# A bias laid into PSUM by ScalarE, and a 64-row product issued into both halves of the array

## The chip, the cores and the metric

The kernel runs on one core of a Trainium2 chip. The core has TensorE (PE: matmuls; its weight loads are the rows PEld), VectorE (DVE), ScalarE (ACT), GpSimd (POOL) and SyncE (SP, which here issues all DMAs). The metric is the device time of one execution in microseconds (us), as the median of the runs: 431.13 us before the change.

## What is computed

Eight batches of 576 rows. An attention through 32 learned memories gives x; x goes through a gated MLP whose gate is mixed over the rows of the sequence by a 576 x 576 matrix and gets a bias per row:

```python
attn_out = softmax(scale * q @ k_m.T) @ v_m            # k_m, v_m: 32 memories per head
x = attn_out.transpose(0, 2, 1, 3).reshape(8, 576, 512)
h = relu(x @ w_in);  u, v = h[..., :512], h[..., 512:]
v_n = (v - mean(v)) / sqrt(var(v) + 1e-6)              # over the 512 columns
v_s = einsum('ts,bsd->btd', w_spatial, v_n) + b_spatial[None, :, None]
out = (u * v_s) @ w_out
```

The change is in the line of `v_s`, the spatial product, and in the order in which all work is issued.

## The kernel before

**Precision.** The large products are made of a high and a low part of each operand (hi x hi, hi x lo, lo x hi), each part in a 32-bit format that TensorE streams in one pass. So a product costs three matmuls where one would be written. Tiles with the suffix h or l (`vh`, `vl`, `wth`, `wtl`, `gh`, `gl`, `woh`, `wol`) are such parts.

**Stages of a batch.** Every stage is a Python generator, and each `yield` ends one step. A letter names the stage:

- P (`memory_weights`) and K (`memories`) make the memories of the batch; S (`scores`) the attention weights `ah`, `al`; Q loads and turns the queries; M (`products`) multiplies the memories by w_in and gives `mh`, `ml`.
- V (`gate`, five row tiles) makes the rows of v, normalises them and leaves `vh`, `vl`. The last tile has only 64 rows (`SR`): its high part goes into rows 0 to 63 of `t1`, its low part into rows 64 to 127 of `t1`, and its high part once more into rows 0 to 63 of `t2`.
- U (`units`, four column tiles of 128) makes u. Each takes 12 matmuls of 288 columns into one double bank of PSUM.
- G (`spatial`, four column tiles) makes the spatial product into a double bank `ps`: the 576 output columns stand as 2 x 288, one half (`hf`) in each bank. Over four tiles of 128 rows stand 3 products x 2 halves = 24 matmuls. The 64 rows that remain take two products of 128 rows each: (`t1`, `ws1`) is hi x hi and lo x hi at once, since `ws1` holds the transposed weights twice; (`t2`, `ws2`) is hi x lo in rows 0 to 63, and in rows 64 to 127 the bias: `t2` is all ones there and `ws2` holds the bias's high part in row 64 and its low part in row 96, zeros elsewhere. That makes 28 matmuls a tile. The first starts the accumulation (`start=(n == 0)`). DVE then multiplies u by `ps` (line 689), and ACT and DVE split the product into `gh`, `gl` and the 64 remaining rows' `grh`, `grl`.
- O (`project`) multiplies by w_out: 12 matmuls of 512 columns a tile; the 64 remaining rows of two batches go together in every second batch.

Steps that happen once: D loads w_in (64-bit floats, which `decode` turns to 32 bits in the stages E and L), X does the same with w_out (`prepare_out`), W loads w_spatial (`load_spatial`), T transposes it on TensorE (`transpose_spatial`; its fifth tile, T4, fills `ws1` and `ws2`), and B (`prepare_bias`) puts the bias into `ws2`.

**Order.** Nothing is scheduled by the compiler: `START` and `PLAN` are lists of letters, each a step of its stage, and every engine runs its instructions in that order (`tc.manual_schedule`). `START` is written out once, for the first batch; `PLAN` is repeated for batches 1 to 7, and a prime means the next batch, two primes the one after. An engine whose next instruction waits therefore holds up all that stands behind it.

**PSUM.** `ps1` has four single banks, `ps2` two double banks. All tiles `pu` and `ps` share the two double banks, so a G tile can start only when an earlier tile's bank has been read out, by ACT (u, line 649) or by DVE (g, line 689).

**Shapes on TensorE.** The profile names a matmul by the rows and columns of the array that it uses. Most are 128\*128 (or 128\*64 for V's last tile). K, S and M use eight small tiles of 64\*32 at once, in both halves of the rows and in four groups of columns. A matmul of plain 32-bit floats in K, S and M shows as two instructions in the trace. A matmul with 64 rows and 128 columns (64\*128) stands only in T, where the last 64 rows of w_spatial are transposed (line 287).

Of the kernel before, what the change touches and what calls it, by code (L numbers as in the profile page):

```python
# [39 lines left out]

PLAN = """
    U0 P'*3 K' P' V1 V0 U0 K' U0 K' V2 U2 V0 V1*3 U1 V2 V0 V2 V0 V4 U1 V1 V0 V2 K' Q' P'' V1 U1
    V3 U3 Q' U2 V1 V4*2 K' V2 P'' K'*2 P'' V3 P'' K' P'' V3 V4 K' K'' U3 K' S' U2 U3 V2 V4 S' V3
    S' V3 S'*2 G0 V4 G1 P'' M0' Q'' P'' M1' M0' S' V3 V2 S' M1'*2 G0 V4 G1 G0 V3 S' G1 V4 G0 P''
    M1' S' M0' Q G1 G0 M1' G0 S' G1 S' M1' K'' P'' G0 S' Q'' G1 G0*2 M0' G2 G3 P'' G2 S' G3 G1*3
    G2 G3 G2*3 M1' G3 O3 G2 S' G3 S'*2 O0 G3 S' O1 G3 O0 S' G3 P'' M0' S' O3 O0 G2 O0 G3 O1 O3
    M0' O3 O4 G2 Q'' O2 M0' O1 O4 O1 V0' O2 O4*2 Q'' O2 V0' O2
"""

ON_VECTOR = set(  # L50
# [7 lines left out]
def memory_attention_spatial_gate(  # L58
# [75 lines left out]
    nc.gpsimd.memset(t2[SR:P, :].bitcast(F32), 1.0)  # L134
# [5 lines left out]
    ws2 = const.tile([P, S], F32R, name="ws2")  # L140

    state = {}

# [6 lines left out]
    def tensor_unless(name):  # L150
        return None if name in ON_VECTOR else nc.tensor
# [81 lines left out]
        yield from decode(w, state["raw", c][n], w, power, f"{'LE'[c]}{n}")  # L233

    def prepare_out(b, j):
        place = two.tile([P, 1, 3 * DM], I32, tag="raw_out", name="raw_out")
        raw, f = place[:, :, 0 : 2 * DM], place[:, :, 2 * DM :].bitcast(F32)
        nc.sync.dma_start(raw[:, 0], w_out[j * P : (j + 1) * P].bitcast(I32))
        yield
        power = two.tile([P, 1, DM], I32, tag="o", name="power")  # L240
        yield from decode(None, raw, f, power, f"X{j}")
        if ("wo", j // 2) not in state:
            state["wo", j // 2] = tuple(
                one.tile([P, 2, DM], F32R, tag=f"{part}{j // 2}", name=part)
                for part in ("woh", "wol")
            )
        woh, wol = (x[:, j % 2] for x in state["wo", j // 2])
        w = raw.rearrange("p j (f t) -> p j f t", t=2)[:, 0, :, 1].bitcast(F32)
        nc.scalar.copy(woh, w)
        yield  # L250
        engine(f"X{j}.wol").tensor_tensor(wol, w, woh.bitcast(F32), op=ALU.subtract)
        yield

    def load_spatial(b, _):
        w_sb = one.tile([P, NI, S], F32, tag="u", name="w_sb")
        w_rem = two.tile([SR, S], F32, tag="g", name="w_rem")
        b_sb = two.tile([P, S], F32, tag="g", name="b_sb")
        state["spatial"] = w_sb, w_rem, b_sb
        nc.gpsimd.memset(b_sb[SR:P], 0.0)
        nc.sync.dma_start(w_sb, w_spatial[0:SM].rearrange("(i p) s -> p i s", i=NI))  # L260
        nc.sync.dma_start(w_rem, w_spatial[SM:S])
        for r in (64, 96):
            nc.sync.dma_start(b_sb[r : r + 1], b_spatial.rearrange("(o s) -> o s", o=1))
        yield
        w_dup = one.tile([P, NI, 2, SR], F32, tag="grh", name="w_dup")
        w_rem_dup = one.tile([SR, 2, SR], F32, tag="grl", name="w_rem_dup")
        state["dup"] = w_dup, w_rem_dup
        for c in range(2):
            nc.scalar.copy(w_dup[:, :, c, :], w_sb[:, :, SM:S])
            yield  # L270
            nc.scalar.copy(w_rem_dup[:, c, :], w_rem[:, SM:S])
            yield

    def transpose_spatial(b, si):
        w_sb, w_rem, _ = state["spatial"]
# [29 lines left out]
    def prepare_bias(b, _):  # L305

        b_sb = state["spatial"][2]
        nc.scalar.copy(ws2[SR:P], b_sb[SR:P])
        yield
        nc.gpsimd.tensor_tensor(  # L310
            ws2[96:97], b_sb[96:97], ws2[96:97].bitcast(F32), op=ALU.subtract
        )
        yield


    def over_rows(eng, to, op):

# [257 lines left out]
    def gate(b, st):  # L575
# [78 lines left out]
    def spatial(b, dt):  # L654
# [10 lines left out]
        rc = slice((b % 2) * SR, (b % 2 + 1) * SR)  # L665
        ps = banks(f"ps_{b}_{dt}")
        cs = slice(dt * P, (dt + 1) * P)
        ops = []
        for i in range(NI):
            ops += [  # L670
# [1 line left out]
                (vh[:, i, cs], wtl[:, i, :]),  # L672
                (vl[:, i, cs], wth[:, i, :]),
            ]
        ops += [(t1[:, cs], ws1), (t2[:, cs], ws2)]
        for n, (a, w) in enumerate(ops):
            for hf in range(2):
                nc.tensor.matmul(  # L678
                    ps[:, hf, 0:HALF],
                    a,  # L680
                    w[:, hf * HALF : (hf + 1) * HALF],
                    start=(n == 0),
                    stop=(n == len(ops) - 1),
                )
            if n in (2, 5, 8):
                yield
# [47 lines left out]
    def warm_up(b, _):  # L734
# [76 lines left out]
```

## Time and profile before

| | before |
|---|---|
| time, median of 3 runs (lowest, highest) | 431.13 us (431.1, 431.83) |
| span of the profiled execution, first to last instruction | 429.2 us |
| PE busy | 399.7 us, 3844 matmuls |
| DVE busy | 292.5 us |
| ACT busy | 228.3 us |
| POOL busy | 81.7 us |
| bytes moved by DMA | 50.69 MB |

The profile gives the span of one execution; the device time of that same execution is not listed beside it. The runs' median is 1.9 us longer than the span, which is what lies before the first and after the last instruction.

How to read it: the page's first part gives busy time, but matmuls are pipelined, and the end of a matmul is modelled, so a PE that is "busy" is not shown to be at its peak. What tells more is the distance between the starts of two matmuls of a stream. In the timeline, neighbouring instructions of one kind are merged into a row: start, time to the end of the last, engine, line, operation, output<-inputs, shape, count. A bracket at the end is idle time of the engine before the row and what ended it. A group's row gives busy time and the mean of one in ns.

### The profile page before, as it was taken

How to read it: one execution, taken by the hardware profiler on the slowest of the kernel's cores; microseconds unless marked ns; L12 is line 12 of the kernel's file. 1: busy time of each engine (PE TensorE's matmuls, PEld its weight loads, DVE VectorE, ACT ScalarE, POOL GpSimd, SP SyncE). 2: the span in 40 equal slices, each digit the busy share in tenths (PEclk: the TensorE clock that was granted, in tenths of full speed). 3: DMA queues.
4: the chain of work that ended last, by engine and by line, in shares of the span. 5: the costliest groups of instructions: out<-in, count | busy, mean ns of one | idle time of the engine just before them, and what ended most of it. 6: DMA issues, size and time to landing. Idle time of an engine off the chain costs nothing.

```text
span 429.2 us, 9278 instructions
## 1 busy us (share of the span) xinstructions
PE 399.7 (93%) x3844; PEld 335.9 (78%) x3844; DVE 292.5 (68%) x536; ACT 228.3 (53%) x438; POOL 81.7 (19%) x154
## 2 busy tenths in 40 slices
PE   3176799999999999999999999999999999999996
PEld 2063487988798887988798887988798888988984
DVE  3699999994997358953897168955897069824420
ACT  2657697654845277245835176245825276337422
POOL 1344353332300031023200030003200040005000
PEclk9999699999999999999999999999999999999999
DMA  8989639217960369014941279025911200020003
GB/s 291 401 296 323 78 99 225 108 48 178 224 93 25 100 197 185 8 73 141 240 34 43 83 210 178 0 76 185 199 30 58 67 2 0 2 98 2 0 2 121
DMA packets 85790, 50.69 MB, mean 118 GB/s; under 512 B 66226, under 2 KB 70322, under 8 KB 85748
## 3 DMA queue, kind: packets, MB, share of 16 engines
q1 hardware_dynamic: 85748, 50.10, 45.3%
q8 instruction: 30, 0.49, 0.5%
q14 instruction: 12, 0.10, 0.1%
HBM read 40.65 MB, written 9.44 MB: 117 GB/s over the span
## 4 chain that ended last, share of the span: by engine, by line
PE 89%; DVE 4%; DMA 3%; ACT 2%; issue 1%; SPq 0%; ACTq 0%; DVEq 0%
PE ps L678 29%; PE po L718 23%; PE pv L591 14%; PE pu L640 12%; PE kvm L375 4%; PE mp L561 4%; PE sc L492 2%; DMA raw<-in_moe_w_in_dram 2%; DMA w_rem<-in_moe_w_spatial_dram 2%; DVE win_sb L218 1%; DVE power L210 1%; DVE sm L512 1%; ACT raw L208 1%; ACT qT L445 0%; DVE g L689 0%
## 5 line engine op out<-in xcount | busy, mean ns | idle before, releaser
L598 DVE BATCH_NORM_STATS2 st<-vr 128x6 f32<-128x512 f32 (+1 forms) x40 | 27.4, 686 | 46.6 <-ACT vr L595 46.6
L678 PE MATMUL ps<-wth,vh 128*128 128x288 f32 x256 | 57.8, 307 | 0.1
L603 POOL TENSOR_SCALAR rs<-mv 128x1 f32<-128x1 f32 (+1 forms) x40 | 11.6, 291 | 236.1 <-DVE mv L600 232.1
L700 ACT CAST gh<-g 128x512 fp32r<-128x512 f32 x32 | 19.9, 621 | 67.9 <-DVE g L689 67.9
L678 PE MATMUL ps<-wtl,vh 128*128 128x288 f32 x256 | 54.9, 296 | 0.0
L678 PE MATMUL ps<-wth,vl 128*128 128x288 f32 x256 | 54.7, 295 | 0.0
L718 PE MATMUL po<-woh,gh 128*128 128x512 f32 x128 | 50.5, 394 | 0.0
L718 PE MATMUL po<-wol,gh 128*128 128x512 f32 x128 | 50.4, 394 | 0.0
L718 PE MATMUL po<-woh,gl 128*128 128x512 f32 x128 | 50.3, 393 | 0.0
L678 PEld LDWEIGHTS ps<-wth,vh 128*128 128x128 f32 x256 | 40.6, 188 | 11.0 <-issue 5.5
L724 ACT COPY o<-po 128x512 f32<-128x512 f32 x36 | 21.1, 587 | 51.5 <-PE po L718 51.5
L678 PEld LDWEIGHTS ps<-wtl,vh 128*128 128x128 f32 x256 | 41.3, 188 | 0.0
L678 PEld LDWEIGHTS ps<-wth,vl 128*128 128x128 f32 x256 | 41.3, 188 | 0.0
L613 ACT ACTIVATE vr<-vr,sh,rs 128x512 f32<-128x512 f32 (+1 forms) x40 | 32.4, 815 | 2.6 <-POOL sh L608 2.3
L591 PE MATMUL pv<-mh,ah 128*128 128x512 f32 (+1 forms) x80 | 32.9, 411 | 0.0
L649 ACT ACTIVATE u<-pu 128x576 f32<-128x576 f32 x32 | 20.2, 659 | 21.8 <-PE pu L640 21.5
L595 ACT ACTIVATE vr<-pv 128x512 f32<-128x512 f32 (+1 forms) x40 | 23.8, 595 | 14.6 <-PE pv L591 14.6
L591 PE MATMUL pv<-ml,ah 128*128 128x512 f32 (+1 forms) x80 | 31.6, 395 | 0.0
L591 PE MATMUL pv<-mh,al 128*128 128x512 f32 (+1 forms) x80 | 31.6, 395 | 0.0
L689 DVE TENSOR_TENSOR g<-u,ps 128x576 f32<-128x576 f32 x32 | 23.9, 750 | 10.8 <-PE ps L678 10.5
L718 PEld LDWEIGHTS po<-woh,gl 128*128 128x128 f32 x128 | 24.0, 188 | 5.7
L718 PEld LDWEIGHTS po<-woh,gh 128*128 128x128 f32 x128 | 24.0, 188 | 5.2
(150 smaller groups left out, 872.2 us busy)
## 6 DMA issues: line engine op xcount, KB each, us to landing
kv_sb<-in_k_dram SPq DMA_DIRECT2D x8, 1152.0 KB, 6.9
kv_sb<-in_v_dram SPq DMA_DIRECT2D x8, 1152.0 KB, 8.9
out_dram<-o SPq DMA_DIRECT2D x32, 256.0 KB, 2.0
q_sb<-in_q_dram SPq DMA_DIRECT2D x28, 288.0 KB, 6.5
phi_sb<-in_phi_dram SPq DMA_DIRECT2D x8, 576.0 KB, 4.1
raw<-in_moe_w_in_dram SPq DMA_DIRECT2D x8, 512.0 KB, 8.1
raw_out<-in_moe_w_out_dram SPq DMA_DIRECT2D x4, 512.0 KB, 3.6
w_sb<-in_moe_w_spatial_dram SPq DMA_DIRECT2D x1, 1152.0 KB, 6.8
```

Source lines behind the costliest of these rows:

```text
L375: nc.tensor.matmul(kvm[r][32 * j : 32 * j + 32], phi_sb[halves[r], j, i, :], kv_sb[halves[r], j, :, i * D : (i + 1) * D], start=(i == 0), ...
L591: nc.tensor.matmul(pv, x[:, r, cs], m[:, r, DM:DFF], start=(n == 0), stop=(n == 5))
L595: nc.scalar.activation(vr, pv, AF.Relu)
L598: nc.vector.bn_stats(st6, vr)
L613: nc.scalar.activation(vr, vr, AF.Identity, bias=sh, scale=rs)
L640: nc.tensor.matmul(pu[:, hf, 0:HALF], m[:, r, cs], a[:, r, hf * HALF : (hf + 1) * HALF], start=(n == 0), stop=(n == 5),)
L649: nc.scalar.activation(u[:, dt, :].rearrange("p (a s) -> p a s", a=2), pu[:, :, 0:HALF], AF.Relu)
L678: nc.tensor.matmul(ps[:, hf, 0:HALF], a, w[:, hf * HALF : (hf + 1) * HALF], start=(n == 0), stop=(n == len(ops) - 1),)
L689: nc.vector.tensor_tensor(g.rearrange("p (a s) -> p a s", a=2), u[:, dt, :].rearrange("p (a s) -> p a s", a=2), ps[:, :, 0:HALF], op=ALU.mult,
L700: nc.scalar.copy(hi, x)
L718: nc.tensor.matmul(po, a, w, start=(n == 0), stop=(n == 11))
L724: nc.scalar.copy(o, po)
```

## The change

Three things, and what they need:

1. **Bias.** The bias is no longer a row of the product. `b_spatial` is loaded into all 128 rows of a new tile `b_all` (a broadcast DMA in `load_spatial`). At the start of each G tile ACT copies it into the double bank, and all matmuls accumulate onto it (`start=False`). The copy is a step of its own. The stage B, the tile `b_sb`, its memset and the memset of ones in `t2` go away.
2. **hi x lo of the remaining 64 rows.** In place of two matmuls of 128 rows with (`t2`, `ws2`), two of 64 rows: half 0 takes rows 0 to 63 of `t1` and `ws2`, half 1 takes rows 64 to 127 of `t2` and `ws2`. `ws2` holds the low part of the weights' left 288 columns in its upper rows and of the right 288 in its lower rows. V's last tile writes `t2` in rows 64 to 127, and T4 writes `ws2` in pieces.
3. **Orders.** `START` and `PLAN` are new. `prepare_out` keeps two buffers for the raw words but only one for `f`.

```diff
@@ spatial
+        nc.scalar.copy(ps[:, :, 0:HALF], b_all.rearrange("p (a s) -> p a s", a=2))
+        yield
         ops = []
...
-        ops += [(t1[:, cs], ws1), (t2[:, cs], ws2)]
-        for n, (a, w) in enumerate(ops):
+        ops += [(t1[:, cs], ws1), None]
+        for n, both in enumerate(ops):
             for hf in range(2):
+                rows = slice(hf * SR, (hf + 1) * SR)
+                if both:
+                    a, w = both[0], both[1][:, hf * HALF : (hf + 1) * HALF]
+                else:
+                    a, w = (t1, t2)[hf][rows, cs], ws2[rows]
                 nc.tensor.matmul(
                     ps[:, hf, 0:HALF],
                     a,
-                    w[:, hf * HALF : (hf + 1) * HALF],
-                    start=(n == 0),
+                    w,
+                    start=False,
                     stop=(n == len(ops) - 1),
+                    skip_group_check=True,
                 )
@@ gate, last tile
-            nc.scalar.copy(t2[0:SR], vr)
+            nc.scalar.copy(t2[SR:P], vr)
@@ load_spatial
-        nc.gpsimd.memset(b_sb[SR:P], 0.0)
...
-        for r in (64, 96):
-            nc.sync.dma_start(b_sb[r : r + 1], b_spatial.rearrange("(o s) -> o s", o=1))
+        nc.sync.dma_start(b_all, b_spatial.rearrange("(o s) -> o s", o=1).to_broadcast([P, S]))
@@ transpose_spatial, T4
-                yield from low(f"wtl{si}{cs.start}", ws2[0:SR, cs], part[0:SR], hi[0:SR])
+                name = f"wtl{si}{cs.start}"
+                if tensor_unless(name):
+                    nc.tensor.matmul(
+                        part, minus, hi, start=False, stop=True, skip_group_check=True
+                    )
+                yield
+                for hf in range(2):
...
+                    if tensor_unless(name):
+                        nc.scalar.copy(to, part[rows, at])
+                    else:
+                        nc.vector.tensor_tensor(
+                            to, part[rows, at], hi[rows, at].bitcast(F32), op=ALU.subtract
+                        )
+                yield
@@ prepare_out
-        place = two.tile([P, 1, 3 * DM], I32, tag="raw_out", name="raw_out")
-        raw, f = place[:, :, 0 : 2 * DM], place[:, :, 2 * DM :].bitcast(F32)
+        raw = two.tile([P, 1, 2 * DM], I32, name="raw_out")
+        f = one.tile([P, 1, DM], F32, name="f_out")
```

Of the orders, the part that a middle batch spends on G and its neighbours, as TensorE meets it when the two lists are read off (x6, x4, x2: matmuls as the kernel writes them; "pair": the two of 64 rows; mb: one transpose of P):

```
before: ... kvm x40, pv1, pu0, kvm x32+8, ... sc, ps0 x6, ps1 x6, mt, mp, mp, ps0 x6, ps1 x6, ps0 x6,
        ps1 x6, ps0 x6+4, ps1 x6+4, mb, ps2 and ps3 in turn by x6, ps2 x6+4, ps3 x6+4, po ...
after:  ... pv1, kvm x40, kvm x32+8, ... ps0 x6, ... sc, ps0 x12, mt, ps1 x12, ps0 x6+2, pair, mp, mp,
        ps1 x6, ps1 x6+2, pair, ps2 x18, ps2 x6+2, pair, mb, ps3 x18, (po1 x6), ps3 x6+2, pair, po ...
```

While `PLAN` runs, the two parts of K stand together in the new order, and the pair of G0 stands directly before M. Over the whole program the lists hold 32 stretches of 64\*32 work before and 25 after, and 32 pairs, of which 6 stand directly before such a stretch.

More of the change, by code (lines that the diff above doesn't have):

```diff
@@ new lines @@
+    T1 T2*2 L1 T1 P L1 E0 L0 P L0 L1 E0 L1 P T2 L1 T0 E0 T4 E0 Q T0 P E0 D1 K*2 L1 T4 X0 Q K*2 L0
+    K*2 Q T4 E0 E1*2 Q*3 P' T4 X0 K Q P' Q*3 E1 K P' K X1 K T0 Q P' Q S E1*2 X0 S*3 M0 P' K' X0 S
+    T0*2 M0 P' T4 P' M0 S M0 P' S E1 P' E1 T4 E1 M0 X0 T4 X0 S P' M0 T3*2 P' K' T3 S T3 M0 T3 M1
+    T3 P' S*3 M1 T0 Q' S M1*2 P' M1 S K' P' M1 P' T0 S K' S T3 S*2 K' U0 S M1 U1 X0*2 V1 Q' V1 V0
+    K' V1 X0 V0 Q' U0 V0 X1 V0 V2 K' Q' K' V3 U0 X0 V2 P'' V1 U1 V0*2 U3 X1 P'' V1 K' V0 V2 X0 X1
+    Q' U1 V4 U2 U3 Q' V1 X1 V1 V4 K' V2 K' V3*3 V4 K' U3 G0 V2 S' U2 P'' S' V2 S'*2 V4 U2 V3 X1
@@ L39 @@
+    G0*2 M0' S' V2 M1' G1 V4 X2 X1*2 M1' X1 G1 V3 V4 P'' X2 X1 G1 X2 V4 G1 V3 M1' V4 X1 X2 G1 X2
+    G0 P'' M1' G1 X2*2 G0 G3 S' X2 X3 P'' M1' G1 P'' M0' M1' K'' Q'' G3 G0 G3*2 G0 G2 X3 G1 G3 X2
+    G1 P'' G0 X3 G2 P'' G2 X3 G0 S' G1 M0' K'' X3 G2 X3 G0 X3 P'' M0' S' M1' X2 X3 P'' G2*3 G3 O3
+    G3 X2 X3*2 G2 M0' X3 G3 S' G3 S' P'' O1 S' G2 O2 O3 S' O3 S'*2 O1 S'*3 O2 M0' O3 P'' M0' O2
+    O0 O2 S'*2 O0 O1 O0 P'' O0 G3 P'' G2 O1
 """
 PLAN = """
[L42 removed]
@@ L48 @@
+    V3 U2 P'' G0 U0 V4 U0 V3 V1 G0 Q' V4 K'*3 U3 V3 V2 V3 V4 Q U3 V3 S' P''*2 K'' U3 Q'' P'' V2
+    P'' V4 V3 G0 S'*2 G1 V4 G0 V4 S' P'' V4 P'' S' G1 V4 G1 G0 M1' M0' S' G0 M0' M1' S' M0' G2 G1
+    G0 G1 P'' G1 S' G1 G0 M0' G2 K'' S' G2 G1 G2 G0 G1 M1'*2 G2 M0' G1 P'' S' G2 G3*4 M1' M0' P''
+    S' G2 O1 G3 O3 G0 M1' G2 S' G3 S' G3*2 G2 O1*2 G3 Q'' M1' O3 S'*2 O3 S' O2 O1 O3 O2 O4 M0' G2
+    S'*3 O0 G3 V0'*2 O2 O4 P'' Q''*2 O0 O2 O0 O4 O0 O4
 """
@@ L133, in memory_attention_spatial_gate @@
     t2 = const.tile([P, 512], F32R, name="t2")
-    nc.gpsimd.memset(t2[SR:P, :].bitcast(F32), 1.0)
+    b_all = const.tile([P, S], F32, name="b_all")
     win_sb = const.tile([P, NJ, DFF], F32, name="win_sb")
@@ L139, in memory_attention_spatial_gate @@
     ws1 = const.tile([P, S], F32R, name="ws1")
-    ws2 = const.tile([P, S], F32R, name="ws2")
+    ws2 = const.tile([P, HALF], F32R, name="ws2")
     state = {}
@@ L256, in load_spatial @@
         w_rem = two.tile([SR, S], F32, tag="g", name="w_rem")
-        b_sb = two.tile([P, S], F32, tag="g", name="b_sb")
-        state["spatial"] = w_sb, w_rem, b_sb
-        nc.gpsimd.memset(b_sb[SR:P], 0.0)
+        state["spatial"] = w_sb, w_rem
         nc.sync.dma_start(w_sb, w_spatial[0:SM].rearrange("(i p) s -> p i s", i=NI))
         nc.sync.dma_start(w_rem, w_spatial[SM:S])
-        for r in (64, 96):
-            nc.sync.dma_start(b_sb[r : r + 1], b_spatial.rearrange("(o s) -> o s", o=1))
+        nc.sync.dma_start(b_all, b_spatial.rearrange("(o s) -> o s", o=1).to_broadcast([P, S]))
         yield
@@ L302, in transpose_spatial @@
             else:
-                yield from low(f"wtl{si}{cs.start}", ws2[0:SR, cs], part[0:SR], hi[0:SR])
[L305 to L313, printed above, removed]
+                name = f"wtl{si}{cs.start}"
[6 more added lines that the diff above has]
+                    rows = slice(hf * SR, (hf + 1) * SR)
+                    first = max(cs.start, hf * HALF)
+                    count = min(cs.stop, (hf + 1) * HALF) - first
+                    if count <= 0:
+                        continue
+                    at = slice(first - cs.start, first - cs.start + count)
+                    to = ws2[rows, first - hf * HALF : first - hf * HALF + count]
+                    if tensor_unless(name):
[5 more added lines that the diff above has]
+                yield
     def over_rows(eng, to, op):
@@ L674, in spatial @@
             ]
-        ops += [(t1[:, cs], ws1), (t2[:, cs], ws2)]
-        for n, (a, w) in enumerate(ops):
+        ops += [(t1[:, cs], ws1), None]
+        for n, both in enumerate(ops):
             for hf in range(2):
+                rows = slice(hf * SR, (hf + 1) * SR)
+                if both:
+                    a, w = both[0], both[1][:, hf * HALF : (hf + 1) * HALF]
+                else:
+                    a, w = (t1, t2)[hf][rows, cs], ws2[rows]
                 nc.tensor.matmul(
```

23 lines of the change are left out of this document (4 added, 19 removed).

## The prediction

> **What bounds the kernel now.** I read the page first, then busy time by stretches, then the chain that ended last. The chain's view gives start, length and work of each piece; here stand its pieces of one batch's G stage and the end.
>
> ```profile
> PE 399.7 (93%) x3844; PEld 335.9 (78%) x3844; DVE 292.5 (68%) x536; ACT 228.3 (53%) x438; POOL 81.7 (19%) x154
> PE 89%; DVE 4%; DMA 3%; ACT 2%; issue 1%; SPq 0%; ACTq 0%; DVEq 0%
> 0.00:50.00 50.00, 24.55 (x346) 15.21 (x354) 37.82 (x51) 29.67 (x57) 18.30 (x22) 0.94 0.94 298
> 112.00:161.00 49.00, 49.00 (x482) 41.69 (x480) 34.27 (x66) 24.81 (x48) 6.82 (x17) 1.00 0.54 118
> 163.17 1.80 PE ps L678 x12
> 165.07 1.88 PE mp L561 x32
> 173.12 7.66 PE ps L678 x56
> 425.36 0.59 ACT o L724
> ```
>
> PE holds 89% of the chain. In a middle stretch (112 to 161 us; columns: length, busy time of PE, PEld, DVE, ACT, POOL, clock, DMA share, GB/s) PE is busy for all 49 us at full clock, DVE for 34, ACT for 25. Only the first 50 us are otherwise: there PE works half the time, DVE 38 us, and the DMAs 94%. So from about 52 us to 425 us the time is the sum of what PE streams, and an ns more or less there is an ns of the kernel. A busy PE might still wait, so I measure the stream itself, by starts.
>
> ```profile
> 174.23 0.43 PE L678 MATMUL ps<-wtl,vh 128*128 128x288 f32 x2
> 178.77 0.69 PE L678 MATMUL ps<-ws,t 128*128 128x288 f32 x4
> 173.49 0.43 PE L678 MATMUL ps<-wth,vl 128*128 128x288 f32 x2
> 173.86 0.30 PEld L678 LDWEIGHTS ps<-wth,vh 128*128 128x128 f32 x2 [0.17 <-DVE g L689]
> 173.86 0.53 PE L678 MATMUL ps<-wth,vh 128*128 128x288 f32 x2
> ```
>
> Between the first two rows' starts stand 34 matmuls: 4.54 / 34 = 0.133 us, the price of one 288-column slot. The last three rows show what a wait costs: after two slots from 173.49 the next should start at 173.76. Its bank was read out late by DVE's g; it starts at 173.86, and its pair lasts 0.53 in place of 0.43, because its weight load, else hidden behind the matmul before, stands open for 0.10. So a wait of PE costs at least 0.2 us. Waits of this kind are few:
>
> ```profile
> PEld ps L678 <- DVE g L689: 1.6, 8, 0.3
> ```
>
> Eight in all, 1.6 us. The old order leaves PE next to nothing to win except by streaming less.
>
> **The pair, on PE.** Per G tile two slots go: 2 x 0.133 = 0.267 us. Two matmuls of 64 rows come. Whether they run side by side, and what it costs to change the array's shape, the trace shows in other shapes.
>
> ```profile
> 161.61 0.42 PE L640 MATMUL pu<-ah,ml 128*128 128x288 f32 x2
> 161.97 0.47 PE L492 MATMUL sc<-qT,kT 64*32 64x288 f32 x8
> 163.09 0.30 PEld L678 LDWEIGHTS ps<-wth,vh 128*128 128x128 f32 x2 [0.47 <-ACT u L649]
> 163.10 0.54 PE L678 MATMUL ps<-wth,vh 128*128 128x288 f32 x2
> 27.92 0.66 PE L287 MATMUL wt<-ident,w_dup 128*128 128x128 f32 x4
> 28.50 0.27 PE L287 MATMUL wt<-ident,w_rem_dup 64*128 64x64 f32 x1
> 28.50 0.14 PEld L287 LDWEIGHTS wt<-ident,w_rem_dup 64*128 64x128 f32 x1 [0.17 <-issue]
> 28.70 0.31 PEld L443 LDWEIGHTS tq<-ident,q_all 128*128 128x128 f32 x3
> 28.71 0.55 PE L443 MATMUL tq<-ident,q_all 128*128 128x128 f32 x3
> 32.73 0.27 PE L454 MATMUL tq<-ident,q_all 128*128 128x128 f32 x1
> 32.84 0.27 PE L455 MATMUL tq<-ident,q_all 128*64 128x128 f32 x1
> 32.95 0.27 PE L454 MATMUL tq<-ident,q_all 128*128 128x128 f32 x1
> ```
>
> - *Side by side: yes.* The eight `sc` matmuls, four in each half of the rows, all start and end inside 0.47 us. The two of the pair write different banks, as those do. I take one slot and a few ns, 0.14 us.
> - *Changing the rows costs.* After `pu` at 161.61 the next slot would be 161.88; `sc` starts at 161.97, 0.09 late, and nothing was waited for. The fourth transpose of the 27.92 row starts at 28.58 - 0.27 = 28.31, and such a transpose takes 0.11 (the rows at 32.73 and 32.84), so 28.42 would be next; the 64\*128 one, of just the pair's shape, starts its weight load at 28.50, after 0.08 to 0.09 of "issue". On the way back: 28.50, plus its open load (0.05), plus 64 columns at half of 0.11 (0.05), is 28.60; the next load starts at 28.70, 0.10 later. So it is 0.09 each way, in which not even the weights are loaded.
> - *Changing the columns alone costs nothing*: 128\*128 and 128\*64 alternate at 0.11.
> - *The load stands open.* On return from `sc` the first pair takes 0.54 in place of 0.43: 0.11 for a load in the format of the G stage. The load of the pair has as many columns, so 0.11 as well, if its two loads run side by side.
>
> A pair alone: 0.09 + 0.11 in, 0.14, 0.09 + 0.11 out = 0.54 us, where 0.267 went: **0.27 us more per tile**. Bounds: without any price for the change of shape the pair saves 0.267 - 0.14 = 0.13; with the halves one after another it costs another 0.13, together 0.40 more.
>
> The page "TensorEngine Tiling (Array Packing)" of the Trainium skill, section Key Properties, says that a change of the tiling mode drains TensorE, without a figure; the trace has 0.09 each way.
>
> **The orders, on PE.** 26 of the 32 pairs stand alone: 26 x 0.27 = 7.0 us. Six stand directly before M. There the way out is shared: what is added is 0.20 in and 0.14, less 0.267, 0.07, if the change from 64\*128 to 64\*32 costs like any other: 6 x 0.07 = 0.4 (if it costs nothing, M's own way in is saved as well, and the six come to nothing). Seven stretches of 64\*32 work go, since K's parts stand together:
>
> ```profile
> 147.33 0.42 PE L640 MATMUL pu<-ah,ml 128*128 128x288 f32 x2
> 147.69 1.37 PE L375 MATMUL kvm<-kv_sb,phi_sb 64*32 64x128 f32 x80
> 148.99 0.50 PE L591 MATMUL pv<-mh,ah 128*128 128x512 f32 x1
> ```
>
> From 147.33 + 0.27 = 147.60 to 148.99 + 0.10 (the open load: 0.50, where its neighbours take 0.40) are 1.49 us. The 80 instructions, eight at a time and 128 columns each at 0.11, make 1.09. So a stretch costs 0.40 beside its work, and seven fewer save 2.8 us. Sum on PE: 7.0 + 0.4 - 2.8 = **+4.6 us**.
>
> **The bias copies.** 32 copies of 128 x 576 into PSUM on ACT; no row shows ACT writing PSUM.
>
> ```profile
> L649 ACT ACTIVATE u<-pu 128x576 f32<-128x576 f32 x32 | 20.2, 659 | 21.8 <-PE pu L640 21.5
> L541 ACT CAST ah<-aT 128x576 fp32r<-128x576 f32 x16 | 10.8, 673 | 7.9 <-DVE aT L537 6.7 <-DVE den L397 0.7 <-DVE aT L535 0.4
> L700 ACT CAST gh<-g 128x512 fp32r<-128x512 f32 x32 | 19.9, 621 | 67.9 <-DVE g L689 67.9
> ```
>
> By the nearest, u of the same shape, 0.66 us: 21 us more for ACT, 53% to 58%. The added wait is ACT's: the copy waits for the bank, with `gh`, `o`, `vr` and the exponent queued behind it, and PE waits for the copy. Price of the copy on the path: 0 if it ends before PE gets there; 0.66 and a wait (0.2) if not. Read off the lists: the copies for G0 and G1 stand after the u that frees their bank; that for G2 waits for G0's g, while PE has M and G1 (about 4.5 us); that for G3 waits for G1's g, and ACT has before it two `gh`, the exponent (1.17), `cmb`, two small copies and one `mh`, some 4 us, while PE streams G2's 26 slots and a pair, 26 x 0.133 + 0.54 = 4.0. That is tight, and I take 0: the eight waits of 0.2 that stood at the same place before pay for a small miss.
>
> **The rest.** `b_all` brings 128 x 2304 B = 0.295 MB into a stretch in which the DMAs are full, ahead of most of w_in, which the chain passes:
>
> ```profile
> 8.90 7.46 DMA raw<-in_moe_w_in_dram
> 15.00:20.00 5.00, 0.00 (x0) 0.00 (x0) 3.31 (x6) 2.43 (x4) 0.00 (x0) 1.00 1.05 391
> 25.00:30.00 5.00, 4.68 (x171) 4.08 (x155) 4.97 (x9) 0.74 (x4) 2.23 (x2) 1.00 0.55 187
> ```
>
> At 391 GB/s that is 0.75 us; what follows is DVE's work (4.97 of 5 us), which starts later by as much: +0.7 us. The new START's other moves I can't price; in it stand the same DVE steps before the first U and V, with part of X0 moved ahead, so between 2 us less and 2 more, and I take 0. The memsets, B, T4's extra pieces, and `f`'s single buffer are POOL's (19% busy) or a few hundred ns of engines ahead of a saturated PE: 0; were DVE's share of T4 uncovered it would be under 0.5. The end is the same `o` and its DMA: 0.
>
> **Sum.** +4.6 + 0.7 = +5.3. On the profiled execution: span 429.2 to 434.5; with the 1.9 us by which the median exceeds the span, **436.4 us**. What a measurement of this kernel can tell from no change is about 0.2%, 0.9 us.
>
> **Rivals.**
>
> 1. *The pair costs one slot and nothing else* (faster). Decided at the first pair: does the matmul after it start 0.13 later or 0.33? Then 32 x 0.13 = 4.2 less, 2.8 less for K, 0.7 more: 424.8 us. For it speaks `sc`, which does run in both halves at once; against it each change of rows in the trace, the 64\*128 one included. Chance 0.12. The page "TensorE: Matmul & The Clock Gate" of the Trainium skill, Part 3, section Measured speedup vs the span model, has packed matmuls take one matmul and about 4 ns for each further tile; by that alone one would expect this rival. The trace agrees inside a stretch (eight `sc` matmuls in 0.47 us), not at its edges.
> 2. *The shape costs, the loads are hidden.* 0.09 + 0.14 + 0.09 = 0.32: 26 x 0.05 = 1.4, the six -0.04 each, -2.8, +0.7: about 430.2. For it: nothing; all returns show the open load. A START better by a few us would end here too. Chance 0.13.
> 3. *The bias copy comes late on ACT.* Each batch G3 waits for one more ACT operation (0.62, `gh`) and the refill (0.2): 8 x 0.8 = 6.6 on top, 443 us. For it: the tight count above; against it: ACT is idle for 67.9 us ahead of `gh`, so that it is seldom behind. Chance 0.10.
> 4. *The halves run one after another*: 32 x 0.13 = 4.2 on top, 440.6. Against it: `sc`. Chance 0.05.
>
> **How the numbers follow.** Forecast 0.60, with its own range of 433 to 440 (START's 2 us, six merged pairs, small misses). The range reaches from 429, which takes in rival 2, to 442.5, which takes in rival 4 and part of 3; rival 1 and the rest of 3 stay out. Faster: rival 1 and some of 2, 0.20. Same: some of 2 and the forecast's edge, 0.08. Slower: 0.72.
>
> **What would show it.** In the changed profile: line of the pair with 64\*128 rows x64; the load of the matmul after each pair 0.09 after the pair's end and open for 0.11; 0.54 us from the last 128-row slot to the first full one. `kvm` in one stretch of 144 instructions and more. A new ACT group of 32 near 0.66 us, and no wait of `ps` for it above 2 us in all. G in a middle batch 4 x 0.27 longer, less 0.2 for the one beside M. The first `pu` near 53 us. It would be wrong if weights load during the change of shape, if TensorE takes the pair in its 128-row shape, or if START moves the first `pu` by several us.

## The result, and the profile after

| | before | after |
|---|---|---|
| time, median (lowest, highest) | 431.48 us (431.1, 432.08), 4 runs | **437.79 us** (435.37, 438.77), 4 runs |
| ratio to before | 1 | **1.0135**, 95% interval 1.0104 to 1.0167 |
| span of the profiled execution | 429.2 us | 436.7 us (its own time: 438.49 us) |

The change makes the kernel 6.3 us slower. The forecast was 436.4, of 429.0 to 442.5. The sum is close; its terms are not, as the stretches show. (The profiled execution of after lies 0.7 us above its median, so the two spans differ by 7.5 us.)

From the page after, its row of busy times and its chain by engine (the same two rows of before stand in the prediction):

```profile
PE 406.0 (93%) x3844; PEld 334.1 (76%) x3844; DVE 290.8 (67%) x537; ACT 248.2 (57%) x469; POOL 81.9 (19%) x151
PE 83%; DVE 7%; ACT 3%; DMA 2%; POOL 1%; issue 1%; SPq 1%; ACTq 0%; DVEq 0%; POOLq 0%
```

ACT has the expected 20 us more (31 instructions more), and still 43% of its time free. What the page says beyond that: PE's share of the chain fell from 89% to 83%, and DVE's and ACT's rose. PE lost its sole hold on the end somewhere, and the chain's share doesn't say where. So I cut the span at three starts that both kernels have: the first `pu`, the first `po` and the last `po`. The timeline of before, then of after:

```profile
52.47 0.40 PE L640 MATMUL pu<-ah,mh 128*128 128x288 f32 x1
85.12 0.48 PE L718 MATMUL po<-woh,gh 128*128 128x512 f32 x1
424.88 0.40 PE L718 MATMUL po<-woh,gl 128*128 128x512 f32 x1
```

```profile
54.35 0.40 PE L647 MATMUL pu<-ah,mh 128*128 128x288 f32 x1
89.04 0.50 PE L734 MATMUL po<-woh,gh 128*128 128x512 f32 x1
431.15 0.39 PE L734 MATMUL po<-woh,gl 128*128 128x512 f32 x1
```

| stretch | before | after | difference | forecast |
|---|---|---|---|---|
| start to first `pu` | 52.47 | 54.35 | +1.9 | +0.3 (load +0.7, one stretch of 64\*32 work less -0.4) |
| first `pu` to first `po` (batch 0) | 32.65 | 34.69 | +2.0 | +1.1 (4 pairs) |
| first to last `po` (the stream) | 339.76 | 342.11 | **+2.35** | +4.0 (28 pairs, six joined K) |
| last `po` to the end of the span | 4.32 | 5.56 | +1.24 | 0 |

The forecast's terms are put here to the stretch in which their matmuls stand; both kernels have the same matmuls in each stretch, but for the pairs. The stream grew by little more than half of what was forecast for it; the start and the end gave the rest.

**The pair itself**, in the groups kept apart by shape and in the timeline of a middle batch after:

```profile
L693 PE MATMUL ps<-ws,t 64*128 64x288 f32 x64 | 12.8, 397 | 0.0
L676 ACT COPY ps<-b_all 128x576 f32<-128x576 f32 x32 | 20.7, 648 | 2.7 <-DVE g L705 2.1
171.79 0.63 PE L693 MATMUL ps<-ws,t 128*128 128x288 f32 x3
172.34 1.95 PE L568 MATMUL mp<-win_sb,vT 64*32 64x512 f32 x32
185.28 0.76 PE L693 MATMUL ps<-ws,t 128*128 128x288 f32 x4
185.97 0.50 PE L734 MATMUL po<-woh,gh 128*128 128x512 f32 x1
186.30 0.40 PE L734 MATMUL po<-wol,gh 128*128 128x512 f32 x1
```

The row at 185.28 merges two full slots and the pair. Single records give what it hides: from the last full slot to the pair 0.224 us (0.133 for the slot, 0.091 for the change of shape; 32 of 32 between 0.222 and 0.225); between the two halves 3 ns; from the second half to the next start 0.327. Here: 185.28 + 0.133 + 0.224 = 185.64, and 0.33 later stands `po` at 185.97, lasting 0.50 in place of 0.40: its load is open for 0.10. Together 0.091 + 0.003 + 0.327 + 0.107 - 0.266 = **0.262 us a pair, where 0.27 was forecast**. The row at 171.79 has one full slot and the pair, and `mp` at 172.34 is again 0.33 behind it: from 64\*128 to 64\*32 is a change like any other.

PE's waits between 110 and 430 us (engine, line, releaser: us, times, longest), before and after, the rows that concern G:

```profile
PEld ps L678 <- issue: 5.0, 6, 0.8
PEld ps L678 <- DVE g L689: 1.4, 7, 0.3
```

```profile
PEld ps L693 <- issue: 12.4, 40, 0.8
PEld ps L693 <- ACT ps L676: 0.9, 2, 0.7
PE ps L693 <- ACT ps L676: 0.2, 1, 0.2
```

The rows named "issue" rose by 34 times and 7.4 us, 0.22 each: the pairs' edges. The waits for DVE's g went away, which the forecast had left standing. The waits for the bias copies are three, 1.1 us in all.

### The profile page after: what moved, and what is told of

It reads as the page before. It is cut to its first block, busy times and chain, and to the rows that moved or that the text cites. A ratio compares the mean times of both kernels' runs of the same rounds, so it can differ in the third digit from the quotient of the medians.

```text
span 436.7 us, 9314 instructions
## 1 busy us (share of the span) xinstructions
PE 406.0 (93%) x3844; PEld 334.1 (76%) x3844; DVE 290.8 (67%) x537; ACT 248.2 (57%) x469; POOL 81.9 (19%) x151
## 4 chain that ended last, share of the span: by engine, by line
PE 83%; DVE 7%; ACT 3%; DMA 2%; POOL 1%; issue 1%; SPq 1%; ACTq 0%; DVEq 0%; POOLq 0%
PE ps L693 29%; PE po L734 23%; PE pv L598 10%; PE pu L647 10%; PE mp L568 4%; PE kvm L382 3%; DMA raw<-in_moe_w_in_dram 2%; PE sc L499 2%; DVE power L210 1%; DVE win_sb L218 1%; DVE st L605 1%; ACT vr L602 1%; DVE power L187 1%; ACT vr L620 1%; POOL rs L611 1%
## 5 line engine op out<-in xcount | busy, mean ns | idle before, releaser
L610 POOL TENSOR_SCALAR rs<-mv 128x1 f32<-128x1 f32 (+1 forms) x40 | 13.5, 338 | 260.1 <-DVE mv L607 247.5
L577 ACT CAST mh<-mp 128x512 fp32r<-128x512 f32 x32 | 18.2, 588 | 25.7 <-PE mp L568 25.7
L598 PE MATMUL pv<-mh,ah 128*128 128x512 f32 (+1 forms) x80 | 31.7, 397 | 0.0
L647 PE MATMUL pu<-ah,mh 128*128 128x288 f32 x128 | 29.2, 309 | 0.0
```

The source lines that it names most:

```text
L577: nc.scalar.copy(mh[:, r, cs], mps[r])
L598: nc.tensor.matmul(pv, x[:, r, cs], m[:, r, DM:DFF], start=(n == 0), stop=(n == 5))
L647: nc.tensor.matmul(pu[:, hf, 0:HALF], m[:, r, cs], a[:, r, hf * HALF : (hf + 1) * HALF], start=(n == 0), stop=(n == 5),)
```

## The experiments

Times are compared with runs of the kernel before on the same chip (medians 431.44 to 431.85 us). The stretches come from the starts in each run's trace, as above.

| | median us (lowest, highest; runs) | ratio, 95% | first `pu` | first `po` | stream | end |
|---|---|---|---|---|---|---|
| before | 431.48 | 1 | 52.47 | 85.12 | 339.76 | 4.32 |
| after | 437.79 (435.37, 438.77; 4) | 1.0104 to 1.0167 | 54.35 | 89.04 | 342.11 | 5.56 |
| e1 | 433.66 (431.66, 434.15; 8) | 1.0026 to 1.0056 | 54.25 | 88.86 | 337.45 | 5.56 |
| e2 | 440.83 (440.15, 441.11; 4) | 1.0198 to 1.0227 | 54.74 | 89.00 | 344.26 | 5.54 |
| e3 | 449.25 (448.57, 449.66; 5) | 1.0395 to 1.0426 | 54.82 | 89.09 | 353.99 | 4.39 |
| e4 | 430.06 (429.11, 430.44; 6) | 0.9949 to 0.9976 | 52.95 | 85.38 | 338.03 | 4.32 |
| e5 | 437.98 (436.82, 438.23; 4) | 1.0131 to 1.0161 | 54.60 | 89.30 | 341.60 | 5.55 |
| e6 | 438.08 (435.91, 439.49; 6) | 1.0125 to 1.0173 | 55.04 | 89.72 | 342.10 | 5.55 |
| e7 | 436.06 (434.75, 437.3; 6) | 1.0093 to 1.0129 | 51.84 | 86.48 | 342.07 | 4.41 |
| e8 | **428.36** (427.37, 428.8; 5) | 0.9908 to 0.9937 | 53.62 | 86.12 | 336.38 | 4.32 |
| e9 | 434.32 (431.58, 435.75; 8) | 1.0029 to 1.0085 | 54.00 | 86.43 | 342.17 | 4.33 |
| e10 | 440.99 (440.77, 442.5; 5) | 1.021 to 1.0245 | 55.31 | 89.95 | 343.51 | 5.56 |
| e11 | **427.81** (427.28, 428.13; 4) | 0.9891 to 0.9921 | 51.32 | 85.49 | 336.39 | 4.33 |
| e12 | 436.15 (435.29, 436.59; 4) | 1.0076 to 1.0111 | 52.20 | 87.15 | 342.10 | 5.57 |

The stream's column is the steady one: after, e6, e7 and e12 have the same order there and agree within 0.04 us, while their first `pu` spreads over 3.2 us. A small effect in the stream is read from that column, not from the medians.

### e1: the new orders without the pair

The rest's second product is again two matmuls of 128 rows, with `ws2` zero in its lower rows; bias copies and orders stay. To make room, `vmn` shares a buffer with `cmb`, and T4 writes `ws2` in one step as before.

```diff
-        ops += [(t1[:, cs], ws1), None]
+        ops += [(t1[:, cs], ws1), (t2[:, cs], ws2)]
```

> The changed kernel with the pair alone undone: the remaining rows' hi x lo is again two matmuls of 128 rows (the lower 64 rows of the weights are zeros), the bias copy and the new orders stay; one small tile shares another's buffer to make room. Theory (a pair that stands alone costs 0.26 us on TensorE, one beside M 0.06): 26 x 0.26 + 6 x 0.06 = 7.1 us less than the changed kernel, 430.7 us, about the time of the kernel before. Rival (the pair hardly costs, since a batch in the middle grew by 0.1 us only; the loss is the first 110 us and the end): within 1 us of the changed kernel, 437 us. In the trace: no 64*128 rows in G, and the slot after each tile follows at 0.13.

433.66 us, 4.1 less than after: between the theory and the rival. The stream is 4.66 us shorter, 0.17 for each of its 28 pairs, not 0.26. The reason is in e1's waits in the same window:

```profile
PEld po L715 <- DVE gl L699: 2.0, 5, 0.4
```

These are new: without the pair PE comes to the projection before DVE has made `gl`. So in the changed kernel part of the pairs' price seems to be time in which PE would have waited.

### e2: the old START, with half the bias

START of before with the bias copies put in; `b_all` holds the left 288 values and both halves of the columns get them, so the right half has a wrong bias. `f` has its two buffers again.

```diff
-        nc.sync.dma_start(b_all, b_spatial.rearrange("(o s) -> o s", o=1).to_broadcast([P, S]))
+        nc.sync.dma_start(b_all, b_spatial[0:HALF].rearrange("(o s) -> o s", o=1).to_broadcast([P, HALF]))
```

> The changed kernel with the list of the first batch from the kernel before (the bias copies put in behind the steps that free their banks, the stage B left out), the new list for the later batches. So that the old list can run, the loads of w_out keep two buffers for f, and the bias tile holds only the left 288 values, which both halves get: the right half's bias is not the right one. Theory (the first batch's order costs 4.3 us less the 1.0 of its four pairs): about 3.3 us less than the changed kernel, 434.5 us, and the scores of batch 2 start 3 us earlier. Rival (the broadcast of the bias, the pairs and the copies hold the first batch up, whatever its order): 437 us.

Both missed: 440.83. The start wasn't regained: first `pu` 2.3 us later than before, although START is the old one. The chain of e2 in its first 18 us shows one part of it:

```profile
7.86 10.04 DMA raw<-in_moe_w_in_dram
17.90 0.03 issue
```

In the kernel before, the same block of w_in ended at 8.90 + 7.46 = 16.36. Now it ends at 17.90, 1.5 us later, for a broadcast of 0.147 MB, half of the change's. The clock differs too: 0.62 of full speed in 50 to 55 us, 0.93 in before. The stream is 2.15 us longer than after's as well, though PLAN is the same; 1.4 of it has come by the end of the first batch of PLAN, so the seam between the old START and the new PLAN is the likely place. I did not follow it further.

### e3: both old orders

As e2, with PLAN too that of before, and G's copy put behind each step that frees its bank. Bias as in e2.

```diff
-    V0*3 V2 P'*2 U1 ...            (after's PLAN)
+    U0 P' P' P' K' P' V1 V0 ...    (before's PLAN, with one more G behind the U or G that frees the bank)
```

> As the run before, with both lists from the kernel before: pair and bias copies in the old order, K in two parts, every pair alone. Theory: the kernel before plus 32 x 0.26 = 8.4 us, less up to 1.6 where a pair's refill falls together with an old wait for a bank: 438 to 440 us. Rival (the pair hardly costs, the orders do): 431 to 433 us.

449.25, ten above the theory. Waits of PE between 110 and 430 us:

```profile
PEld ps L694 <- ACT ps L677: 11.3, 23, 0.9
PE ps L694 <- ACT ps L677: 4.2, 9, 0.6
```

So the mechanism of rival 3 is real: in the old order the copy comes late on ACT at 23 weight loads, three of the four tiles in most batches (the nine matmuls wait at the same places). In the new order the same view has three such waits. This is what the new PLAN is needed for.

### e4 and e8: the kernel before, with K joined, then with G2 joined

e4 puts the two parts of K side by side, as the change does; e8 also lets PE stream more of G2 before it turns to G3's bank, whose read-out PE waited for.

```diff
-    U0 P'*3 K' P' V1 V0 U0 K' U0 K' ...
+    U0 P'*4 V1 V0 U0 K'*2 U0 K' ...
-    ... M0' G2 G3 P'' G2 S' G3 G1*3
+    ... M0' G2*2 P'' G3 S' G3 G1*3      (e8 only)
```

> The kernel before with one edit: in the list of the later batches the first part of K stands directly before the second. Theory (a stretch of 64*32 work costs 0.40 us beside its work): 6 x 0.40 = 2.4 us less than before, 429 us. Rival (the later first part holds up the memories, and PE waits for them or for the gate's tiles): no change, 431.5 us.

> The kernel before with K joined as in e4, and in the list of the later batches G2 takes its first 12 matmuls before G3 starts, where the two took turns by six. Theory (G3's start waits each batch for G1's bank, 0.21 us of stream in e4's trace, and comes 0.8 us later now): 8 x 0.21 = 1.7 us less than e4, 428.4 us. Rival (the wait moves on to another tile): 430 us.

e4: 430.06, stream -1.73. One joining is worth what the forecast said; before (the row at 147.69 in the prediction, and these) and e4:

```profile
151.02 0.42 PE L640 MATMUL pu<-ah,ml 128*128 128x288 f32 x2
151.37 1.16 PE L375 MATMUL kvm<-kv_sb,phi_sb 64*32 64x128 f32 x64
152.27 0.30 PE L387 MATMUL kvm<-ones,es 64*32 64x2 f32 x16
152.49 0.50 PE L591 MATMUL pv<-mh,ah 128*128 128x512 f32 x1
```

```profile
149.62 0.42 PE L640 MATMUL pu<-ah,ml 128*128 128x288 f32 x2
149.97 2.25 PE L375 MATMUL kvm<-kv_sb,phi_sb 64*32 64x128 f32 x144
151.96 0.30 PE L387 MATMUL kvm<-ones,es 64*32 64x2 f32 x16
152.19 0.50 PE L591 MATMUL pv<-mh,ah 128*128 128x512 f32 x1
```

Before: 1.49 for the first part, and 151.02 + 0.27 = 151.29 to 152.49 + 0.10 = 152.59, 1.30, for the second: 2.79. e4: 149.89 to 152.29, 2.40. That is 0.39. The stream has six such places, 2.3 us, and shows 1.73; where the other 0.6 went I haven't found.

e8: 428.36, stream another -1.65, and the row "PEld ps <- DVE g" is gone from its waits. In the stream that is seven waits of the eight (the other is START's), 0.24 us each, worth their full length, and a list of letters is all it takes. **e8 is 0.9923 of before (0.9908 to 0.9937) and faster than both kernels.**

### e5: no bias copy

The bias is left out of the sum, and the first matmul starts the accumulation.

```diff
-        nc.scalar.copy(ps[:, :, 0:HALF], b_all.rearrange("p (a s) -> p a s", a=2))
-                    start=False,
+                    start=(n == 0),
```

> The changed kernel without ScalarE's 32 bias copies: the first matmul of a tile starts the accumulation, and the bias is left out of the sum (its load stays). Theory (the copies end before TensorE gets there; the changed trace has PE wait for them about 1 us in all): 0 to 1 us less, 437 to 437.8 us. Rival (ScalarE, busy 20 us more, holds up what is queued behind the copies): 2 us less or more, below 436 us.

437.98, no change; the stream is 0.51 us shorter. 32 copies of 0.648 us cost half a microsecond: PE's few waits for them.

### e6: the bias loaded late

```diff
@@ load_spatial
-        nc.sync.dma_start(b_all, ...)
@@ memory_weights
+        if b == 2:
+            nc.sync.dma_start(b_all, ...)
```

> The changed kernel with one DMA moved: the broadcast of the bias is issued behind the load of batch 2's phi, at about 55 us, in place of ahead of w_in. Theory (the broadcast takes 2 us of the full DMA stretch at the start, seen in the last of the six first blocks of w_in, which lands at 18.3 in place of 16.4 us): first u tile 1.9 us earlier, 436 us or a little less. Rival (the new order of the first batch makes it late by itself): first u tile at 54.3 us as before, 437.8 us.

438.08, no gain, and the first `pu` at 55.04. The data did come earlier: the last of the first six w_in blocks landed at 16.69 us, in after at 18.33. But this profile had a lower clock (0.66 in 30 to 40 us, after 0.83), so its first `pu` alone decides nothing. The runs do: at like mean clocks those of e6 and of after lie together (at 0.984, 438.2 and 439.0 against 438.5; at 0.988, 436.8 and 437.9 against 437.1 and 438.8). In the new START the broadcast isn't worth the 1.9 us of the theory, though it delays w_in there as in the old one (e2).

### e7: the end of PLAN

```diff
-    ... O0 O2 O0 O4 O0 O4
+    ... O0 O2 O4 O0 O4 O0
```

> The changed kernel with the last six steps of the list of the later batches in another order: the tile of the remaining rows (two DMAs) is copied out and stored before the last full tile (one DMA). Theory (the new list ends with two copies and three DMAs one behind the other): from the last matmul's start to the end of the span 4.3 us in place of 5.6, 436.6 us. Rival (the end hangs on the DMA's own 2 us and the closing steps): no change, 437.8 us.

The end is 4.41 us in place of 5.56, as expected: the new PLAN closes with the projection of the 64 remaining rows, whose two copies and three DMAs come behind the last `po`. The stream is the same (342.07). Its first `pu`, in a START that is unchanged, came at 51.84, 2.5 us earlier than in after's profile. That asked for another cause in the start, and e9 to e12 look for it: the granted clock of 45 to 55 us is 0.86 in e7's profile and 0.56 in after's.

### e9 and e10: matmuls that nobody reads, in PE's pauses

e9 is e8 with six groups (Z) of four 128x128 matmuls in START, e10 the changed kernel with nine.

```diff
+    def warm_up(b, _):
+        while True:
+            idle = bank("idle")
+            for _ in range(4):
+                nc.tensor.matmul(idle[:, 0:P], ident, ident, start=True, stop=True)
+            yield
-    ... S P' T3 E1 M0 E1 P' M0 T3 ...
+    ... S P' T3 E1 M0 Z Z Z Z Z Z E1 P' M0 T3 ...      (e9)
```

> The kernel before with both joins (K' with K', G2 with G2: 428.36 us) plus six groups of four 128x128 matmuls onto a PSUM bank that nobody reads, put into the start order behind the second subtraction of batch 0's means, where TensorE stands idle from about 41 to 44.3 us. Theory (the first 55 us are set by the granted clock, which is low there because TensorE pauses): the clock of 30 to 55 us rises from 0.80 to 0.9 or more, the first pu matmul comes at 52 us or before instead of 53.6, and the time is about 427.2 us. Rival (VectorE, busy without a break at 40 to 50 us, bounds this stretch whatever TensorE's clock): first pu unchanged within 0.4 us, 428.4 us. If the added matmuls are themselves in the way, 429 or more.

> The changed kernel plus nine groups of the same unread 128x128 matmuls in its start order, in the pauses that its profile shows at 22 to 55 us (three behind the first transposition, one behind mb, three behind the weights' transpositions, two behind the second subtraction). Theory (the clock costs the changed kernel's start): clock of 30 to 55 us from 0.73 to 0.9 or more, first pu at about 52 us instead of 54.35, time about 435.5 us. Rival (the clock is not the cause, the copies of data into place are): first pu unchanged, 437.8 us; if the added matmuls are in the way, 439 or more.

Both went slower, and both had a full clock up to 55 us. The timelines say why this isn't the theory's end. e8, then e9:

```profile
44.26 0.79 PE L159 MATMUL wt<-wth,minus 128*128 128x512 f32 x1 [3.29 <-ACT wth L298]
48.42 2.39 PE L375 MATMUL kvm<-kv_sb,phi_sb 64*32 64x128 f32 x80
53.62 0.59 PE L640 MATMUL pu<-ah,mh 128*128 128x288 f32 x2
```

```profile
44.09 3.84 PE L739 MATMUL idle<-ident 128*128 128x128 f32 x32 [1.08 <-DVE phi_sb L350]
47.68 0.48 PE L160 MATMUL wt<-wth,minus 128*128 128x512 f32 x1
50.36 1.37 PE L376 MATMUL kvm<-kv_sb,phi_sb 64*32 64x128 f32 x80
54.00 0.54 PE L641 MATMUL pu<-ah,mh 128*128 128x288 f32 x2
104.27 0.24 PE L388 MATMUL kvm<-ones,es 64*32 64x2 f32 x10
108.21 0.28 PE L388 MATMUL kvm<-ones,es 64*32 64x2 f32 x6 [3.68 <-issue]
109.01 0.63 PE L592 MATMUL pv<-ml,ah 128*128 128x512 f32 x1
```

The added matmuls waited 1.08 us for DVE, which had still to read their bank, and so came at the end of the pause, not into it: the transposed weights start at 47.68, not 44.26. From there to `pu` it takes 6.3 us, not 9.4, and the same 80 `kvm` take 1.37, not 2.39. So the 3 us that the low clock costs here were won and lost again. And a new loss came in the stream (the last three rows), told of below. e10 was misplaced likewise: from the weights (49.77) to its `pu` (55.31) it needs 5.54 us, against 9.28 in after, but gets there later.

### e11 and e12: the same, short enough

Three matmuls of 512 columns in e8's pause (e11), one in the changed kernel's (e12).

```diff
-            for _ in range(4):
-                nc.tensor.matmul(idle[:, 0:P], ident, ident, start=True, stop=True)
+            nc.tensor.matmul(
+                idle.rearrange("p (a s) -> p a s", a=4), ident, ident[:, None, :].to_broadcast([P, 4, P]), start=True, stop=True
+            )
```

> e8 (428.36 us) with three 128x512 matmuls of the identity onto spare banks that nobody reads, behind the second subtraction of batch 0's means: at the 0.24 us per 128 columns that e9's took, 2.9 us, which end at about 44.0, before the transposed weights release TensorE at 44.26. In e9 the stretch from that release to the first pu matmul took 6.3 us at full clock, against 9.4 us in e8, but the added work ended 3.4 us too late. Theory (the low granted clock costs e8 3 us there, and the misplaced work took them back): first pu at about 50.7 us, 425.4 us. Rival (other engines bound this stretch, and e9's was short only because they had run ahead meanwhile): first pu within 0.5 us of 53.6, 428.4 us.

> The changed kernel with one such 128x512 matmul (1.0 us) in its pause of 43.5 to 45.1 us, and none elsewhere. From the release at 45.07 to the first pu it takes 9.28 us in the changed kernel's profile, where the clock is low to the end, 7.18 in that of e7, where it comes back at 48.5, and 5.54 in e10, where it is never low. Theory (the clock): 5.5 to 6 us, first pu at about 51 us, 434.5 us. Rival (the clock falls for the earlier pause at 30 us, or this stretch is bound otherwise): no change, 437.8 us.

After (two rows of the timeline, and a stretch as in the prediction: PE, PEld, DVE, ACT, POOL, clock, DMA share, GB/s), then e12:

```profile
45.07 0.79 PE L159 MATMUL wt<-wth,minus 128*128 128x512 f32 x1 [1.53 <-ACT wth L295]
49.64 2.39 PE L382 MATMUL kvm<-kv_sb,phi_sb 64*32 64x128 f32 x80
45.00:55.00 10.00, 9.82 (x186) 5.99 (x187) 8.04 (x21) 5.83 (x13) 1.27 (x2) 0.56 0.42 45
```

```profile
45.93 0.50 PE L159 MATMUL wt<-wth,minus 128*128 128x512 f32 x1 [0.47 <-ACT wth L295]
49.35 1.37 PE L382 MATMUL kvm<-kv_sb,phi_sb 64*32 64x128 f32 x80
45.00:55.00 10.00, 9.20 (x200) 5.75 (x198) 9.26 (x22) 6.77 (x14) 2.14 (x2) 1.00 0.85 112
```

With one matmul of 1.1 us that nobody reads, the clock of 45 to 55 us is 1.00 in place of 0.56. From the weights to `pu` e12 needs 52.20 - 45.93 = 6.27 us, not 9.28. Its first `po` is 1.9 us earlier than after's, its median 1.6 us lower, and its runs lie within 1.3 us, not 3.4. The theory holds for e12; its size was overestimated by half: the whole prologue before 45 us ran 0.9 us later in this execution (at 35 us already 0.8, ahead of the added matmul). The runs agree. Those of e12 have mean clocks of 0.992 to 1.000, those of after 0.984 to 0.992, and at 0.992 both take the same (435.85 and 435.37).

e11 shows the theory and the rival both: `pu` at 51.32 in place of 53.62, but then PE waits.

```profile
44.27 1.12 PE L738 MATMUL idle<-ident 128*128 128x512 f32 x2 [1.17 <-DVE phi_sb L350]
51.32 0.54 PE L641 MATMUL pu<-ah,mh 128*128 128x288 f32 x2
54.26 0.59 PE L416 MATMUL tk<-ident,kmn 128*128 128x128 f32 x2 [0.56 <-ACT kmn L403]
```

Its first `po` is only 0.63 us earlier than e8's, and 427.81 against 428.36 is not clearly apart from e8. In the old START other engines stand right behind the clock.

## Why the sum was right and its terms were not

**The bound.** "An ns more or less there is an ns of the kernel" held: the stream of e4 and e8 gave most of what their lists should (1.73 of 2.3 us, and 1.65), and that of after, e6, e7 and e12 is the same to 0.04 us. It held less in START, where PE waits.

**The pair.** Right, from rows of `sc` and of T's transposes: side by side (3 ns), 0.091 in, an open load of 0.107 both ways, 0.262 against 0.27. With that rivals 1 (0.13 less after each pair), 2 (hidden loads) and 4 (one half after the other) are out. What the page "TensorE: Matmul & The Clock Gate" of the Trainium skill (Part 3, section Measured speedup vs the span model) gives for packed matmuls, one matmul and a few ns, is what the halves show between them; the edges are what decides here.

**PE's +4.6.** Here the forecast failed in its terms. Of the 4.6, +4.0 belong to the stream; it grew by 2.35, and the runs divide that:

- K joined: -1.73 (e4) where the forecast's seven had -2.8; six lie in the stream, and a single one measures 0.39 against 0.40.
- "The eight waits of 0.2 that stood at the same place before pay for a small miss": this step was wrong. They didn't pay for a miss; the new order takes them away, and that is worth -1.65 on the old kernel (e8). They should have stood as a gain in the sum, since the lists of the change section show G2 streamed in 18 and more before G3.
- e1, with the new order and the copies and no pair, has a stream of 337.45, 1.07 above e8. The copies are 0.51 of it, if they cost there what e5 shows beside the pair; the rest could be its waits for `gl`.
- The pairs: +4.66 (e1 to after). By rows 22 x 0.262 + 6 x 0.07 = 6.2. The 1.5 less fit e1's waits for `gl` (2.0 us), which the pairs fill; that is argued, not shown.

The sum -1.73 - 1.65 + 1.07 + 4.66 = 2.35 is exact by construction; that the parts are of these causes rests on e4, e8, e5 and e1.

**The bias copies.** Costed at 0, and e5 agrees (0.5 in the stream). The tight count for G3 was rightly a concern: in the old order (e3) 23 weight loads wait for copies. Rival 3 is out for the new order only.

**START: +1.4 forecast up to the first `po`, +3.9 came.** This is the largest miss. "START's other moves I can't price ... I take 0", with 2 us either way. Two causes:

- *The granted clock.* e12's first `po` is 1.9 us ahead of after's (87.15 against 89.04). But the old START has a low clock too: 0.71 for 45 to 55 us in before, 0.56 in e8. What differs is its price: in the old START the full clock of e11 wins only 0.63 us at the first `po`. The runs show the same: in before those with a mean clock of 0.982 take 1.2 us longer than those with 0.992 (432.1 and 430.9), in e6, with after's START, 0.980 and 0.995 lie 3.6 us apart (439.49 and 435.91). With a full clock from 40 us on in both, e12's first `po` is 1.66 us behind e11's, where after's is 3.9 behind before's; so some 2.3 us go with the clock, on one profile each. The forecast read the clock of before as an average over 0 to 50 us, 0.94, and asked no further.
- *The place of batch 1's scores.* 2.0 us lie between the first `pu` and the first `po`: 34.6 to 35.0 us in e1, e5, e6, e7 and e12 as in after, so none of pair, copies and load alone makes them. Most of it stands at one place. The timeline of before, then of after:

```profile
68.16 1.20 PE L492 MATMUL sc<-qT,kT 64*32 64x288 f32 x32
69.29 0.53 PE L678 MATMUL ps<-wth,vh 128*128 128x288 f32 x2
```

```profile
67.43 1.36 PE L499 MATMUL sc<-qT,kT 64*32 64x288 f32 x16
69.32 0.87 PE L499 MATMUL sc<-qT,kT 64*32 64x288 f32 x16 [0.53 <-ACT vr L602]
70.12 0.54 PE L647 MATMUL pu<-ah,mh 128*128 128x288 f32 x2
```

From the first score to the next product PE takes 1.13 us in before and 2.69 in after: it comes to the scores before they are ready, a weight load of the first half waits for DVE, and the second half for ACT. That is 1.56 of the 2.0, and it is the list's doing: every run with the new START has 2.67 to 2.70 there, every run with the old one 1.13. The remaining 0.4 isn't divided. The four pairs had been given 1.1 in this stretch; without them (e1) it is no shorter, while the old list with pairs and copies (e2, e3) needs 34.3, 1.6 more than before.

The +0.7 for the broadcast itself was too small for what it does to w_in (1.5 us in e2 for half the bytes, 1.6 in the new START), and in the new START that delay doesn't show in the time (e6).

**The end: 0 forecast, +1.24 came.** "The same `o` and its DMA" overlooked that PLAN's last letters had changed places. e7 changes them back and gets 1.15. It was in the lists to read.

So the sum of 5.3 came close to the median's 6.3 by luck: a stream too dear by 1.6 stood against a start too cheap by 2.5 and an end too cheap by 1.2. The direction hung on the pair's price, and that was read well.

## What to carry to other kernels

A shape that saves streamed columns is paid at its edges: before splitting a saturated product into row tiles, read from any other change of shape in the same trace what a way in and out costs, and compare it with the slot that is saved (here 0.39 against 0.13). If the orders are rewritten with it, make the sum over every wait that the old order had, also those that go away, and read the first and last tokens of the list by themselves; the lists alone, on the old kernel, were worth 3.1 us here. Cut spans at starts that all kernels have: an unsteady start of 3 us hides a stream that repeats within 0.04 us.

## What the runs showed of the hardware

- **Sparse work of PE can halve its clock for the next 3 to 10 us, and the pause that stands just ahead need not be the reason.** After's clock in two stretches (columns as in the prediction, the clock third from the end):

```profile
40.20:43.60 3.40, 1.98 (x9) 0.99 (x8) 3.37 (x4) 3.05 (x7) 0.85 (x1) 1.00 0.91 120
43.60:47.00 3.40, 1.93 (x15) 0.68 (x17) 3.35 (x6) 3.38 (x6) 2.51 (x2) 0.50 1.02 132
```

  It fell at 43.60 and came back at 53.84; the 80 `kvm` in between took 2.39 us, against 1.37 at full clock. The pause of 1.53 us ahead of the row at 45.07 began at 43.54, so it had lasted only 0.06 us when the clock fell: what PE did before counted, and from 40.2 to 43.6 it was busy for 1.98 of 3.40 us, with no pause above 0.9. By the page "TensorE: Matmul & The Clock Gate" of the Trainium skill (Part 1) the array is throttled to half unless it has been busy, and watched over windows of about 3.4 us. The halving agrees, and so do the lengths: every low stretch between 30 and 120 us in these 14 profiles lasts 3.41, 6.83 or 10.24 us. How much work in a window is enough isn't settled here: e7 kept its clock after several stretches of 3.4 us with PE busy for 0.6 of them. Filling a pause pays only if the filler has a free bank and fits (e9 and e10 against e11 and e12).
- **A run of small matmuls may outrun its instructions.** In e9 PE stopped for 3.68 us between two `kvm` matmuls and waited for nothing that the profile shows; in e10 for 1.24, at 158.88 us, at the same work. K's run is 160 matmuls with a load each, 320 instructions. The queue of PE's instructions brings 0.49 MB in 30 transfers for the 7688 of the kernel before, 16 KB or some 256 instructions each. In e9 one of them starts at 104.97 us and takes 1.66; PE goes on 1.6 us after its end. In e10 one starts at 156.45 and takes 0.89; PE goes on 1.5 us after its end. That the pause is this load fits both, but no run moves the one to see the other move. e8 and e11 move the same block near 104 us without a pause. After it e9's clock fell as well (`pv` 0.63 against 0.40), and its stream is 5.8 us longer than e8's; its two runs with a mean clock of 1.00 take 431.6, still 3.2 above e8.
- **A broadcast row is a dear load.** 128 rows of 1152 B from one (0.147 MB) put the w_in behind them back by 1.5 us (e2), the full rows of 2304 B by 1.6 (after against e6), where 0.75 had been given (0.295 MB at 391 GB/s).
